# Sigmoid attention and a SiLU block in one kernel: a quad's seven rounds of values put into one burst between its score tiles

## The chip, the cores and the metric

The kernel runs on one core of a Trainium2 chip. Its time is the device time of one launch in microseconds. A difference is stated against the median of the runs of the kernel before.

## The reference

```python
# q, k, v: (8, 12, 448, 64); w_in: (768, 2048); w_out: (2048, 768)
scores = q @ k.transpose(0, 1, 3, 2) / sqrt(64) - log(448)
attn = sigmoid(scores) @ v                      # (8, 12, 448, 64)
x = attn.transpose(0, 2, 1, 3).reshape(3584, 768)
h = x @ w_in
out = (h * sigmoid(h)) @ w_out                  # (3584, 768), float32
```

## The kernel before

There are two kinds of work, and both are mostly matmuls. The kernel writes the order of every engine's instructions by hand, so what stands in the Python program is the order on each engine.

**Attention.** The twelve heads of a batch are worked in three *quads* of four heads, 24 quads in all. A quad has seven *score tiles* (`scores`): a tile is four matmuls of 64 rows by 64 columns (L178) that run in the four quarters of the array, and one sigmoid of 128x896 on ScalarE (L185) that reads the tile `psc` from PSUM and writes `attnT`. `psc` has two buffers of two banks each (`ps_sc`), `attnT` has twelve. When the quad's tiles are there, its *values* (`values`) follow: seven *rounds* of four 64x64 matmuls (L209) that add up in two PSUM tiles `pav`. After the last round VectorE writes both to `xT` (L225). For odd batches from 3 on, four subtractions `xs` follow on VectorE (L273), two `attnT` buffers are held for them until they are read. `pav` shares the four single banks of `ps_1` with all dense products.

**Dense work.** `h_unit` (batches 0 and 1, tile `ph`) and `h_pair` (batches 2 to 7 in pairs, tiles `hx`, `hy`, `hz`, L320; `hy` is in `ps_sc`) make the hidden layer with 128x128 matmuls. `out_set` makes 256 output rows by seven products `po` of eight matmuls (L465) each; VectorE adds them into `osb` (L475), and ScalarE makes one copy `m` a set (L483). These are generators, chained by `all_moe`: each `yield` hands back the price of one matmul in ns (189 or 163).

**The order.** Score tiles and values are placed by the main loop at the end of the kernel; between them `stretch(ns)` draws dense matmuls from the generator until they have cost `ns`. A run of score and value matmuls between two dense matmuls is called a *burst* here. From tile 42 on (the third batch) there are three *stages*: the tiles of two batches, and four of the next, are spread over the dense work that lies ahead of the next `h_pair`, which itself has no bursts. In a stage the kernel before does this for each pair of tiles:

```python
for u in burst:            # two tiles
    scores(*u)
had = values_if_any()      # the waiting quad's first four rounds, or its last three
rows_if_any()              # one kr or qr copy and its DMA transpose, for a later quad
```

and then a stretch of dense work. Its length is the dense time left in the stage, shared over the bursts left, less 200 ns for each round that the burst had. So a quad's values take two bursts, and the two `pav` tiles stay open over the dense stretch between them. In the last stage the rounds that are left after the last pair make bursts of their own.

`after_values` issues the loads of later `v` rows from POOL, `rows_of_quad` the loads of later `k` and `q` rows and the DMA transposes from SP.

Of the kernel before, what the change touches and what calls it, by code (L numbers as in the profile page):

```python
# [3 lines left out]

# [9 lines left out]
AF = mybir.ActivationFunctionType  # L14
# [4 lines left out]
def kernel(  # L19
# [9 lines left out]
    nc = tc.nc  # L29

    B, H, S, D = q.shape
# [4 lines left out]
    NCH = S // HP  # L36
    NPAIR = H // 2
    NQ = NPAIR // 2
    NT_B = NQ * NCH
    NCC = DMODEL // P  # L40
    NFC = DFF // P
    NO2 = DMODEL // 2
    NQB = NQ * B
    NHC = NFC // 2
# [54 lines left out]
    warm = cpool.tile([P, 1], F32, tag="warm", name="warm")  # L99
# [69 lines left out]
    def scores(g, ch, unread=0):  # L169
        attnT[g, ch] = p12.tile([P, 2, S], F16, tag="attnT", name="attnT")  # L170
        psc = ps_sc.tile([P, 2, 512], F32, tag="pssc", name="psc")
        for _ in range(unread):
            nc.tensor.matmul(psc[:, 0, :P], dummy[:, :P], dummy[:, :P], start=True, stop=True)  # L173
        for half in range(2):
            own = slice(half * HP, (half + 1) * HP)
            for j in range(2):
                rows = slice(j * D, (j + 1) * D)
                nc.tensor.matmul(  # L178
                    psc[own, j, :S],
                    qkT["k", g][rows, ch, own],  # L180
                    qkT["q", g][rows, :, own],
                    start=True,
                    stop=True,
                )
        nc.scalar.activation(  # L185
            attnT[g, ch], psc[:, :, :S], AF.Sigmoid, bias=NEG_LOG_S, scale=QKSCALE
        )
# [3 lines left out]
    h_done = set()  # L191
# [3 lines left out]
    def values(g, end=NCH):  # L195
        b, iq = divmod(g, NQ)
        if b not in xT:
            assert b < 2 or b - 2 in h_done
            xT[b] = p2.tile([P, NPAIR, S], F16, tag="xT", name="xT")
        pav, done_rounds = part_of.pop(g, None) or (  # L200
            [ps_1.tile([P, 512], F32, tag="ps1", name="pav") for _ in range(2)],
            0,
        )
        for ch in range(done_rounds, end):
            at = attnT.pop((g, ch))
            for half in range(2):
                own = slice(half * HP, (half + 1) * HP)
                for j in range(2):
                    nc.tensor.matmul(  # L209
                        pav[half][j * D : (j + 1) * D, :S],  # L210
                        flat["v", g][own, j, ch, :],
                        at[own, j, :],
                        start=(ch == 0),
                        stop=(ch == NCH - 1),
                    )
        if end < NCH:
            part_of[g] = pav, end
            return
        for half in range(2):
            if b > 2 and b % 2 == 1 and iq == NQ - 1 and half == 0:  # L220
                nc.scalar.activation(
                    xT[b][:, half * NQ + iq, :], pav[half][:, :S], AF.Copy, scale=SX
                )
            else:
                nc.vector.tensor_scalar_mul(xT[b][:, half * NQ + iq, :], pav[half][:, :S], SX)  # L225
        if b > 2 and b % 2 == 1:
            x_sums(b // 2, iq)
        if iq == NQ - 1:
            ready.add(b)
# [32 lines left out]
    HCC = NCC // 2  # L262
# [296 lines left out]
    def all_moe():  # L559
        for m in range(B // 2):  # L560
            tail = []
            if m == 0:
                yield from moe_h(0)
                yield from moe_h(1)
                tail = [None, *first_sg]
            else:
                yield from h_pair(m, tail)
            yield from moe_set(m, 0, tail)
            yield from moe_set(m, 2)
            yield from moe_set(m, 4)  # L570
            if m % 2 == 1:
                g = NCH - 1
                yield from out_set(
                    kept,
                    row_blocks(m - 1, g),
                    block(g),
                    row_blocks(m, g),
                    1.0,
                    last=(m == B // 2 - 1),
                )  # L580

    stream = all_moe()
    done = due = 0.0

    def stretch(ns):
        nonlocal done, due
        due += ns
        while done < due or hold:
            step_ns = next(stream, None)
            if step_ns is None:  # L590
                break
            done += step_ns
# [19 lines left out]
    units = [(g, ch) for g in range(NQB) for ch in range(NCH)]  # L612
    waiting = []
# [11 lines left out]
    def after_values(g):  # L625
        if g == 0:
            load("v", 3)
            load_w_in(2)
            load_w_in(3)
        elif g == 1:  # L630
            load("v", 4)
            load_w_out(1, 0)
            load_w_out(1, 1)
        elif g == 2:
            load("v", 5)
            load("kq", 6)
            load_w_out(0, 1)
            load("kq", 7)
            load_w_out(0, 0)
        elif 4 < g < NQB - 3:  # L640
            load("v", g + 3)

    later = []
    seen = cpool.tile([1, 1], F16, tag="seen", name="seen")

    def rows_of_quad(g, name, copy):
        dma_transpose(g, name, copy)
        if name == "q" and g + 3 < NQB:
            nc.gpsimd.tensor_copy(seen, qkT["q", g][:1, NCH - 1, P - 1 :])  # L649
            if g == 6:  # L650
                load("v", 6)
                load("kq", 8)
                load("v", 7)
            load("kq", g + 3)

    def rows_if_any():
        if later:
            rows_of_quad(*later.pop(0), nc.vector.tensor_copy)

    def values_if_any():  # L660
        if not waiting:
            return 0
        g, begin, end = waiting.pop(0)
        rounds(g, end)
        return end - begin
# [10 lines left out]
    def transposes(g, name):  # L676
        pe_transpose(g, ((name, 0, 4), (name, 4, NCH)))
        if name == "q":
            after_transpose(g)

    def rounds(g, end):
        values(g, end)
        if end == NCH:
            after_values(g)
# [31 lines left out]
        for _ in range(4):  # L716
            next(unit)

    PACE, BURST, ROUND, SPARE = 1600, 590, 200, 2400
    sets = 7 * NHC * 163  # L720
    h_at = [(2 * NFC * NCC - 8) * 189 + 3 * sets]
    for m in (1, 2):
        h_at.append(h_at[-1] + 7 * NHC * HCC * 189 + (3 + m % 2) * sets)
    AHEAD = 4
    ends = [2 * NT_B, 4 * NT_B + AHEAD, 6 * NT_B + AHEAD, 8 * NT_B]
    values_left = 2 * NT_B
    stretch(PACE)
    for n in range(NT_B + 3, len(units), 2):
        burst = units[n : n + 2]
        if n == 2 * NT_B:  # L730
            values_if_any()
            stretch(13500)
            later.extend(((8, "k"), (8, "q")))
        for u in burst:
            scores(*u)
        had = values_if_any()
        rows_if_any()
        for g, ch in burst:
            if ch == NCH - 3 and g >= 6 and g % 6 < 4 and g + 3 < NQB:
                later.extend(((g + 3, "k"), (g + 3, "q")))  # L740
            if ch == NCH - 1:
                waiting.extend(((g, 0, NCH),) if n < 2 * NT_B else ((g, 0, 4), (g, 4, NCH)))
        if n in (30, 32):
            transposes(5, "kq"[n // 2 - 15])
        if n < ends[0]:
            stretch(PACE)
            continue
        m = bisect.bisect(ends, n)
        if n + 2 == ends[m]:
            nc.scalar.activation(warm, warm, AF.Silu)  # L750
        dense = h_at[m - 1] - SPARE - done
        due = done
        stretch((dense + values_left * ROUND) / ((ends[m] - n) // 2) - had * ROUND)
        values_left -= had
        if n + 2 == ends[m]:
            while waiting:
                values_if_any()
                stretch(SPARE / 3)
            values_left = 2 * NT_B
            while 2 * m not in h_done:  # L760
                done += next(stream)
            due = done
            stretch(3000)
    for _ in stream:
        pass

# [29 lines left out]
```

## Time and profile before

| | |
|---|---|
| median of 3 runs | 366.58 us (366.13 to 366.73) |
| the profiled execution | 366.59 us |
| its span, first to last instruction | 364.8 us |
| TensorE matmuls, busy | 358.0 us, 98% of the span |
| VectorE, ScalarE, GpSimd, busy | 264.0, 248.3, 63.7 us |
| stages with bursts of the changed loop | about 76 to 123, 159 to 212, 248 to 292 us |

In the rows of the timeline the first number is the start in us from the span's start, the second the time from the first start to the last end of the merged instructions, then engine, line, operation, output and inputs, shape and count; a bracket gives idle time of the engine just before and what ended it. PE is TensorE's matmuls, PEld its weight loads, DVE VectorE, ACT ScalarE, POOL GpSimd, SP the sync engine's queue. Matmuls are pipelined and their ends are modelled, so rows of neighbours overlap.

### The profile page before, as it was taken

To read this page: it belongs to the slowest core of one execution; us is meant where nothing else is said; L and a number is where in the kernel's file an instruction comes from. 1 tells how busy PE (TensorE), PEld (TensorE's weight loads), DVE (VectorE), ACT (ScalarE), POOL (GpSimd) and SP (SyncE) were. 2 spreads that over 40 slices of the span, in tenths; PEclk is the share of its full clock that TensorE was granted. 3 is DMA by queue.
4 is the path that set the end of the run, shared out by engine and by line. 5 is a ranking of instruction groups with operands and counts; after the bars stand their busy time and mean duration, and the time that the engine had idled before them with its cause. 6 is when DMAs were issued, how large, how long until landed. Compare 5 with 4: busy or idle time off the path is not lost.

```text
span 364.8 us, 7652 instructions
## 1 busy us (share of the span) xinstructions
PE 358.0 (98%) x3023; PEld 181.5 (50%) x3023; DVE 264.0 (72%) x497; ACT 248.3 (68%) x362; POOL 63.7 (17%) x105
## 2 busy tenths in 40 slices
PE   8999999999999999999999999999999999999995
PEld 4554445444444555554444455554444455556663
DVE  2574679976888587877668677886867577778773
ACT  4997886787878677587677768658878756660000
POOL 8544310603241002002024101100100000000000
PEclk9999999999999999999999999999999999999999
DMA  8999999999999436307999953812854020003333
GB/s 133 199 205 205 205 204 188 167 185 133 214 156 216 90 81 102 50 0 142 141 173 140 199 115 53 127 25 46 169 78 112 18 71 0 3 0 88 86 86 86
DMA packets 65314, 42.78 MB, mean 117 GB/s; under 512 B 35968, under 2 KB 61824, under 8 KB 65280
## 3 DMA queue, kind: packets, MB, share of 16 engines
q0 software_dynamic: 26944, 22.58, 42.9%
q1 hardware_dynamic: 38112, 19.41, 26.4%
q8 instruction: 23, 0.38, 0.4%
q10 hardware_dynamic: 224, 0.33, 0.2%
q14 instruction: 11, 0.09, 0.1%
HBM read 45.61 MB, written 11.01 MB: 155 GB/s over the span
## 4 chain that ended last, share of the span: by engine, by line
PE 91%; ACT 4%; DVE 2%; DMA 1%; issue 1%; DVEq 0%
PE po L465 36%; PE hy L320 11%; PE psc L178 10%; PE ph L244 9%; PE pav L209 8%; PE hz L320 7%; PE hx L320 7%; ACT attnT L185 4%; DMA qs<-in_q_dram 1%; DVE xs L273 1%; PE ptrq L147 1%; PE ptrk L147 0%; DVE osb L475 0%; PE psc L173 0%; DVE xT L225 0%
## 5 line engine op out<-in xcount | busy, mean ns | idle before, releaser
L185 ACT ACTIVATE attnT<-psc 128x896 f16<-128x896 f32 x168 | 144.1, 930 | 31.7 <-PE psc L178 31.4
L465 PEld LDWEIGHTS <-S 128*128 128x128 f16 x448 | 41.1, 98 | 36.4 <-issue 11.8
L475 DVE SCALAR_TENSOR_TENSOR osb<-po,osb 128x384 f32<-128x384 f32 x70 | 37.6, 554 | 19.4 <-PE po L465 18.8
L178 PE MATMUL psc<-qT,kT 64*64 64x448 f16 x672 | 50.7, 363 | 0.7 <-ACT attnT L185 0.4
L225 DVE TENSOR_SCALAR xT<-pav 128x448 f16<-128x448 f32 x45 | 26.1, 620 | 27.3 <-PE pav L209 27.3
L331 ACT ACTIVATE gTr<-u 128x448 f16<-128x448 f32 x48 | 27.6, 575 | 23.1 <-DVE u L344 19.1
L465 PE MATMUL po<-T,S 128*128 128x384 f16 x224 | 41.6, 327 | 0.0
L465 PE MATMUL po<-w_out_sb,S 128*128 128x384 f16 x224 | 41.5, 327 | 0.0
L209 PE MATMUL pav<-attnT,vf 64*64 64x448 f16 x672 | 41.1, 350 | 0.3 <-DVE gTr L257 0.2
L320 PEld LDWEIGHTS <-w_in_sb 128*128 128x128 f16 x288 | 28.2, 98 | 26.4 <-issue 0.4
L465 PEld LDWEIGHTS <-gTr 128*128 128x128 f16 x304 | 28.0, 98 | 25.6 <-issue 8.6
L244 PE MATMUL ph<-xT,w_in_sb 128*128 128x448 f16 x192 | 38.8, 353 | 0.0
L465 PE MATMUL po<-w_out_sb,gTr 128*128 128x384 f16 x192 | 36.6, 327 | 0.0
L320 PE MATMUL hy<-xs,w_in_sb 128*128 128x448 f16 x144 | 35.1, 352 | 0.1
L320 PE MATMUL hx<-xT,w_in_sb 128*128 128x448 f16 x144 | 34.6, 352 | 0.0
L320 PEld LDWEIGHTS <-W 128*128 128x128 f16 x216 | 21.1, 98 | 19.6
L178 PEld LDWEIGHTS <-kT 64*64 64x64 f16 x672 | 15.8, 104 | 29.5 <-issue 26.9
L84 POOL DMA_DIRECT2D vf<-in_v_dram x24 | 17.0, 712 | 59.0 <-PE pav L209 53.3
L244 PEld LDWEIGHTS <-w_in_sb 128*128 128x128 f16 x192 | 17.6, 98 | 19.4 <-issue 4.1
L475 DVE SCALAR_TENSOR_TENSOR osb<-po,m 128x384 f32<-128x384 f32 x42 | 22.9, 552 | 5.5 <-PE psc L178 2.0
L257 DVE TENSOR_TENSOR gTr<-ph,tsig 128x448 f16<-128x448 f32 x32 | 19.7, 621 | 9.9 <-ACT tsig L256 9.6
L649 POOL COPY seen<-qT 1x1 f16<-1x1 f16 x15 | 3.9, 257 | 127.7 <-DMA qT<-qr 127.7
(75 smaller groups left out, 433.7 us busy)
## 6 DMA issues: line engine op xcount, KB each, us to landing
out_dram<-osb SPq DMA_DIRECT2D x54, 192.0 KB, 3.0
vf<-in_v_dram POOLq DMA_DIRECT2D x24, 224.0 KB, 7.5
kf<-in_k_dram POOLq DMA_DIRECT2D x23, 224.0 KB, 4.9
qf<-in_q_dram POOLq DMA_DIRECT2D x23, 224.0 KB, 7.2
w_in_sb<-in_moe_w_in_dram POOLq DMA_DIRECT2D x8, 384.0 KB, 12.3
w_out_sb<-in_moe_w_out_dram POOLq DMA_DIRECT2D x4, 768.0 KB, 17.3
kT<-kr SPq DMA_TRANSPOSE x18, 4.7
qT<-qr SPq DMA_TRANSPOSE x18, 3.1
```

What stands on the lines that cost most here:

```text
L84: nc.gpsimd.dma_start(flat[name, g][:, :, c0:c1].rearrange("p j c d -> p j (c d)"), rows_in(name, g)[:, :, c0 * D : c1 * D],)
L178: nc.tensor.matmul(psc[own, j, :S], qkT["k", g][rows, ch, own], qkT["q", g][rows, :, own], start=True, stop=True,)
L185: nc.scalar.activation(attnT[g, ch], psc[:, :, :S], AF.Sigmoid, bias=NEG_LOG_S, scale=QKSCALE)
L209: nc.tensor.matmul(pav[half][j * D : (j + 1) * D, :S], flat["v", g][own, j, ch, :], at[own, j, :], start=(ch == 0), stop=(ch == NCH - 1),)
L225: nc.vector.tensor_scalar_mul(xT[b][:, half * NQ + iq, :], pav[half][:, :S], SX)
L244: nc.tensor.matmul(ph[:, :S], w_in_of[:, cc // NQ, cc % NQ, fc * P : (fc + 1) * P], xT[b][:, cc, :], start=(at == 0), stop=(at == NCC - 1),)
L257: nc.vector.tensor_mul(gTr[:, fc, (b % 2) * S : (b % 2) * S + S], ph[:, :S], tsig)
L320: nc.tensor.matmul(ps, a[:, c, i * P : (i + 1) * P], bs(c), start=(first and c == 0), stop=(c == HCC - 1), skip_group_check=True,)
L331: nc.scalar.activation(gTr[:, side * NHC + i, odd * S : (odd + 1) * S], src, AF.Silu, scale=ISX)
L465: nc.tensor.matmul(po[:, :NO2], a[:, fc, :], w[:, fc, :], start=(fc == 0), stop=(fc == NHC - 1))
L475: nc.vector.scalar_tensor_tensor(out=o, in0=po, scalar=sign * scale, in1=x, op0=ALU.mult, op1=ALU.add)
L649: nc.gpsimd.tensor_copy(seen, qkT["q", g][:1, NCH - 1, P - 1 :])
```

## The change

The loop up to tile 42 stays as it was (it is only written out anew). From there on:

- The bursts of a stage are planned ahead by `bursts_to`: two tiles a burst, and three in the burst after the one that holds a quad's last tile. This third kind carries all seven rounds of that quad, between its second and its third tile. Seven tiles make 2 + 2 + 3, three bursts a quad. A burst that only has values follows where the tiles of the kernel have run out.
- Dense work is dealt by tiles: of what is left in the stage a burst gets the share of its tiles among the tiles left, less what the burst itself is priced at (200 ns, and 190 ns for each tile and round).
- `xT`, `xs`, loads and copies are the same instructions; they move with the rounds and bursts that issue them.

```diff
-    PACE, BURST, ROUND, SPARE = 1600, 590, 200, 2400
+    PACE, SWITCH, TILE, ROUND, SPARE = 1600, 200, 190, 190, 2400
...
-        for u in burst:
-            scores(*u)
-        had = values_if_any()
-        rows_if_any()
-        for g, ch in burst:
-            if ch == NCH - 3 and g >= 6 and g % 6 < 4 and g + 3 < NQB:
-                later.extend(((g + 3, "k"), (g + 3, "q")))
-            if ch == NCH - 1:
-                waiting.extend(((g, 0, NCH),) if n < 2 * NT_B else ((g, 0, 4), (g, 4, NCH)))
...
-        m = bisect.bisect(ends, n)
-        if n + 2 == ends[m]:
-            nc.scalar.activation(warm, warm, AF.Silu)
-        dense = h_at[m - 1] - SPARE - done
-        due = done
-        stretch((dense + values_left * ROUND) / ((ends[m] - n) // 2) - had * ROUND)
-        values_left -= had
-        if n + 2 == ends[m]:
-            while waiting:
-                values_if_any()
-                stretch(SPARE / 3)
-            values_left = 2 * NT_B
-            while 2 * m not in h_done:
-                done += next(stream)
-            due = done
-            stretch(3000)
+    def bursts_to(n, stop):
+        bursts, full = [], None
+        while n < stop or full is not None:
+            burst = units[n : min(n + (2 if full is None else 3), stop)]
+            bursts.append((burst, full))
+            n += len(burst)
+            full = next((g for g, ch in burst if ch == NCH - 1), None)
+        return bursts
...
+    for m in range(1, B // 2):
+        stop = min(2 * (m + 1) * NT_B + 4, len(units))
+        bursts = bursts_to(n, stop)
+        n = stop
+        costs = [
+            SWITCH + TILE * len(burst) + ROUND * NCH * (full is not None) for burst, full in bursts
+        ]
+        for at, (burst, full) in enumerate(bursts):
+            if full is None:
+                for u in burst:
+                    scores(*u)
+            else:
+                for u in burst[:2]:
+                    scores(*u)
+                rounds(full, NCH)
+                for u in burst[2:]:
+                    scores(*u)
+            rows_if_any()
+            for g, ch in burst:
+                if ch == NCH - 3 and g % 6 < 4 and g + 3 < NQB:
+                    later.extend(((g + 3, "k"), (g + 3, "q")))
+            if at == len(bursts) - 1:
+                nc.scalar.activation(warm, warm, AF.Silu)
+                break
+            due = done
+            tiles = sum(len(burst) for burst, _ in bursts[at:])
+            left = h_at - SPARE - done + sum(costs[at:])
+            stretch(max(left * len(burst) / tiles - costs[at], 0))
+        while 2 * m not in h_done:
+            done += next(stream)
+        due = done
+        stretch(3000)
+        h_at += 7 * NHC * HCC * 189 + (3 + m % 2) * sets
```

More of the change, by code (lines that the diff above doesn't have):

```diff
@@ L1 @@
-import bisect
 import math
@@ L717 @@
             next(unit)
-    PACE, BURST, ROUND, SPARE = 1600, 590, 200, 2400
[L720 to L725, printed above, removed]
-    values_left = 2 * NT_B
+    PACE, SWITCH, TILE, ROUND, SPARE = 1600, 200, 190, 190, 2400
     stretch(PACE)
-    for n in range(NT_B + 3, len(units), 2):
+    for n in range(NT_B + 3, 2 * NT_B, 2):
@@ L729 @@
         burst = units[n : n + 2]
-        if n == 2 * NT_B:
-            values_if_any()
-            stretch(13500)
-            later.extend(((8, "k"), (8, "q")))
         for u in burst:
             scores(*u)
-        had = values_if_any()
-        rows_if_any()
+        values_if_any()
         for g, ch in burst:
-            if ch == NCH - 3 and g >= 6 and g % 6 < 4 and g + 3 < NQB:
-                later.extend(((g + 3, "k"), (g + 3, "q")))
             if ch == NCH - 1:
-                waiting.extend(((g, 0, NCH),) if n < 2 * NT_B else ((g, 0, 4), (g, 4, NCH)))
+                waiting.append((g, 0, NCH))
@@ L743 @@
         if n in (30, 32):
             transposes(5, "kq"[n // 2 - 15])
-        if n < ends[0]:
-            stretch(PACE)
-            continue
-        m = bisect.bisect(ends, n)
-        if n + 2 == ends[m]:
-            nc.scalar.activation(warm, warm, AF.Silu)
-        dense = h_at[m - 1] - SPARE - done
-        due = done
-        stretch((dense + values_left * ROUND) / ((ends[m] - n) // 2) - had * ROUND)
-        values_left -= had
-        if n + 2 == ends[m]:
-            while waiting:
-                values_if_any()
-                stretch(SPARE / 3)
-            values_left = 2 * NT_B
-            while 2 * m not in h_done:
-                done += next(stream)
-            due = done
-            stretch(3000)
+        stretch(PACE)
@@ new lines @@
+    values_if_any()
+    stretch(13500)
+    later.extend(((8, "k"), (8, "q")))
+    def bursts_to(n, stop):
[6 more added lines that the diff above has]
+        return bursts
+    sets = 7 * NHC * 163
+    h_at = (2 * NFC * NCC - 8) * 189 + 3 * sets
@@ new lines @@
+    n = 2 * NT_B
+    for m in range(1, B // 2):
[28 more added lines that the diff above has]
+            done += next(stream)
+        due = done
+        stretch(3000)
+        h_at += 7 * NHC * HCC * 189 + (3 + m % 2) * sets
```

## The prediction

> **What bounds the kernel now.** I read the page first: the busy shares, the clock row and the chain that ended last.
>
> ```profile
> span 364.8 us, 7652 instructions
> ...
> PE 358.0 (98%) x3023; PEld 181.5 (50%) x3023; DVE 264.0 (72%) x497; ACT 248.3 (68%) x362; POOL 63.7 (17%) x105
> ...
> PEclk9999999999999999999999999999999999999999
> ...
> PE 91%; ACT 4%; DVE 2%; DMA 1%; issue 1%; DVEq 0%
> ```
>
> TensorE is busy 98% of the span, its clock is never cut, and 91% of the chain is matmuls. So the time is the length of TensorE's stream, and a change gains only what it takes out of that stream: matmuls, waits, or lost time between matmuls. The number of matmuls doesn't change here. What is left is the price of going from the dense 128x128 matmuls (`po`) to the 64x64 ones (scores `psc`, values `pav`) and back. For that I read the timeline of TensorE in the second stage with attention, where nothing waits.
>
> ```profile
> 164.33 0.57 PE L178 MATMUL psc<-qT,kT 64*64 64x448 f16 x8
> 164.74 0.93 PE L209 MATMUL pav<-attnT,vf 64*64 64x448 f16 x16
> 165.59 1.31 PE L465 MATMUL po<-w_out_sb,S 128*128 128x384 f16 x7
> 166.84 0.57 PE L178 MATMUL psc<-qT,kT 64*64 64x448 f16 x8
> 167.24 0.74 PE L209 MATMUL pav<-attnT,vf 64*64 64x448 f16 x12
> 167.91 0.34 PE L465 MATMUL po<-w_out_sb,S 128*128 128x384 f16 x1
> 168.08 1.30 PE L465 MATMUL po<-w_out_sb,gTr 128*128 128x384 f16 x7
> 169.31 0.57 PE L178 MATMUL psc<-qT,kT 64*64 64x448 f16 x8
> 169.82 1.64 PE L465 MATMUL po<-w_out_sb,gTr 128*128 128x384 f16 x9
> 171.29 0.65 PE L465 MATMUL po<-T,S 128*128 128x384 f16 x3
> 171.87 0.57 PE L178 MATMUL psc<-qT,kT 64*64 64x448 f16 x8
> ```
>
> The first column is the start. The ends overlap, since matmuls are pipelined, so I use starts alone. Nine `po` matmuls go from 169.82 to 171.29: 1.47 / 9 = 0.163 each. Four 64x64 matmuls (one score tile, or one round of values) run together as a group. Call a group's price G and the price of one burst's two changes C. From 164.33 to 166.84 there are 2 tiles, 4 rounds and 7 dense: 2.51 - 7 x 0.163 = 1.37 = 6G + C. From 169.31 to 171.87 there are 2 tiles and 12 dense: 2.56 - 12 x 0.163 = 0.60 = 2G + C. The difference gives G = 0.19, and C = 0.22. The stretch between them (2 tiles, 3 rounds, 8 dense, 2.47) gives C = 0.21 with that G. So each burst of small matmuls costs 0.22 us beyond its work, whatever lies in it.
>
> Weight loads show what the 0.22 is:
>
> ```profile
> 164.33 0.14 PEld L178 LDWEIGHTS <-kT 64*64 64x64 f16 x8 [0.32 <-issue]
> ```
>
> ```profile
> 165.59 0.93 PEld L465 LDWEIGHTS <-S 128*128 128x128 f16 x7 [0.36 <-issue]
> ```
>
> At both edges the load path stands idle for 0.32 and 0.36 us and waits for nothing: the first load of the other kind isn't taken ahead of the running matmuls.
>
> The Trainium skill ("TensorE: Matmul & The Clock Gate", Part 3, The mechanism) says that a weight load overlaps with running matmuls only where their row groups differ, and a 128-row load meets all of them; the trace agrees, by the idle 0.32 and 0.36 at each edge. The Trainium skill, on the same page under LDWEIGHTS (loading the stationary operand), prices a load at its columns over 1.2 GHz, which would make the two edges 0.05 + 0.11 = 0.16 us, an estimate, and nine bursts 1.4 us; the rows above say 0.22.
>
> **The change part by part.** *Fewer bursts.* From tile 42 on there are 126 score tiles. Before, they come in 63 pairs, the values of a quad ride behind two of them (four rounds, then three), and the last quad's values make two bursts of their own: 65. After, a quad takes a pair, a pair, and a triple with all seven rounds of the quad before between its second and third tile: by the loop 20 bursts in the first stage, 18 in the second, 18 in the third (among them one single tile and one of values alone), 56 in all. The order of TensorE's instructions in the two built programs says the same, 90 and 81 such stretches over the whole kernel. 9 x 0.22 = 1.98 us come out of the stream. The starts are rounded to 0.01, which leaves C between 0.20 and 0.23: 1.8 to 2.1.
>
> *A new crossing, values to scores, inside 17 bursts.* The stages in question have none. The first part of the kernel does:
>
> ```profile
> 22.34 0.38 PE L178 MATMUL psc<-qT,kT 64*64 64x448 f16 x4
> 22.55 0.74 PE L209 MATMUL pav<-attnT,vf 64*64 64x448 f16 x12
> 23.13 0.38 PE L178 MATMUL psc<-qT,kT 64*64 64x448 f16 x4
> ```
>
> Three rounds and the crossing take 23.13 - 22.55 = 0.58, which is three groups of 0.19 and 0.01 over. So 17 crossings cost 17 x 0.01 = 0.2 at most, and I take 0.
>
> *The third tile's buffer.* There are two score buffers, so the third tile of a burst waits until ScalarE has read the first.
>
> ```profile
> 163.02 0.91 ACT L185 ACTIVATE attnT<-psc 128x896 f16<-128x896 f32 x1
> 164.77 1.73 ACT L185 ACTIVATE attnT<-psc 128x896 f16<-128x896 f32 x2 [0.83 <-PE psc L178]
> ```
>
> The sigmoid starts 164.77 - 164.33 = 0.44 after its burst and takes 0.91, so the buffer is free at 1.35. Two tiles and seven rounds take 9 x 0.19 = 1.71: the seven rounds cover the sigmoid with 0.36 to spare. The second sigmoid ends at 0.44 + 1.73 = 2.17, and the third needs about 0.82 more, to 2.99. The next burst follows six to nine dense matmuls later: its first tile at about 9 x 0.19 + 0.19 + 0.22 + 6 x 0.163 = 3.1, its second, which needs the third tile's buffer, at 3.3. Cover remains, 0.3. What eats into it is the 0.50 us copy `m` (L483), one a set, ten in the three stages; here one in the third stage, with the pair that met it:
>
> ```profile
> 276.53 0.64 PE L178 MATMUL psc<-qT,kT 64*64 64x448 f16 x8
> 276.62 0.50 ACT L483 ACTIVATE m<-po 128x384 f32<-128x384 f32 x1
> ```
>
> By the built order of ScalarE four of them come directly ahead of a triple (two in the first stage, two in the third). Each could hold the third tile by 0.50 - 0.36 = 0.14 and the tile after next by 0.2. Bound: 4 x 0.34 = 1.4; below, 0. The pair at 276.53 shows what such a meeting cost before: 0.64 where 0.57 is usual, 0.07. I take 0.2 for all four.
>
> *The waits that the third stage has now.*
>
> ```profile
> 284.91 0.64 PE L178 MATMUL psc<-qT,kT 64*64 64x448 f16 x8
> ...
> 286.05 0.66 PE L465 MATMUL po<-T,gTr 128*128 128x384 f16 x3
> ...
> 288.90 1.39 PE L209 MATMUL pav<-attnT,vf 64*64 64x448 f16 x16
> ...
> 293.72 0.73 PE L320 MATMUL hz<-xs,W 128*128 128x448 f16 x3
> 294.28 0.73 PE L320 MATMUL hx<-xT,w_in_sb 128*128 128x448 f16 x3
> 295.12 0.73 PE L320 MATMUL hy<-xs,w_in_sb 128*128 128x448 f16 x3
> ```
>
> Two pairs (276.53 above and 284.91) take 0.64 for 0.57, 0.14 together, the last quad's first four rounds take 1.39 where 0.93 is usual, 0.46 more, and `hy` comes 0.84 after `hx` where the three matmuls before it took 0.56, 0.28 more. Sum 0.88. The two large ones come from VectorE's queue:
>
> ```profile
> 286.15 1.15 DVE L225 TENSOR_SCALAR xT<-pav 128x448 f16<-128x448 f32 x2 [2.29 <-PE pav L209]
> ...
> 288.75 1.68 DVE L475 SCALAR_TENSOR_TENSOR osb<-po,osb 128x384 f32<-128x384 f32 x3
> ```
>
> After a quad's last round VectorE works off two `xT` and four `xs`, from 286.15 to 288.75, and only then clears the `po` buffers that piled up, which the next values need. Before, the last quad's values come 288.90 - 286.05 = 2.85 us after the end of the quad before. After, the built order has a third tile, 6 dense, a pair, 9 dense, a single, 4 dense between them: 4 groups and 3 C and 19 dense = 0.76 + 0.6 + 3.1 = 4.5 us, more than the same VectorE work (2.6 to 288.75 and three `osb`, 1.68: 4.3). So the 0.46 goes. Behind the last values stand five dense matmuls instead of one ahead of `hx`, 0.65 us more for `xT` and `xs`, so the 0.28 goes too. I take 0.8 of 0.88. If the cover fails, 0.
>
> The same VectorE work now stands behind a whole seven rounds in six quads. But both `pav` buffers are held from their first round to `xT` without a dense stretch in between, 7 x 0.19 = 1.3 us where it was 166.84 - 164.74 + 0.4 + 0.57 = 3.1 us. Two of the four single banks come back sooner for `po`. I take 0 for that, between 0 and 0.5 us.
>
> *Moved along.* The `kr` and `qr` copies and their DMA transposes go one a burst; a quad asks for two and has three bursts (3.5 before), and they are for three quads later. SP's stores and POOL's loads behind them keep their order; the values end a burst earlier, so `vf` loads go out earlier. On the dense side the same 163 ns matmuls are dealt in other portions: 0.
>
> **Sum.** The profiled execution took 366.59 us (span 364.8 and 1.8 around it), as the median of the runs, 366.58. -1.98 - 0.8 + 0.2 = -2.58: **364.0 us**.
>
> **Rivals.** *ScalarE takes part of it back* (chance 0.09): copies and sigmoids in a row hold more third tiles than the four. With the bounds above, +1.4, +0.5 from the `pav` side and the old waits kept in another place (0 instead of -0.8), the sum is 366.59 - 1.8 + 1.9 = 366.7 at the very end; the middle of this case is 365.5. For it, the sum of busy time over the three stages with bursts (76 to 123.5, 159 to 212.5 and 247.8 to 292 us):
>
> ```profile
> sum 145.20, PE 145.13 PEld 69.89 DVE 102.49 ACT 114.16 POOL 25.44; mean PE 48.38 PEld 23.30 DVE 34.16 ACT 38.05 POOL 8.48
> ```
>
> ScalarE is busy 114 of 145 us, so a delay dies out slowly. Against: its work stays the same.
>
> *The third tile waits in every triple* (0.03): slower. It starts where the first sigmoid comes more than 0.36 late, and decides where a triple costs (2.78 + 0.7) / 17 = 0.2 on average. Were each of the 17 late by a whole copy's 0.50 behind a backlog, the third tile would cost 0.14 and the second of the next burst 0.2: 17 x 0.34 = 5.8, and 366.59 - 2.78 + 5.8 = 369.6. Against it: the row at 164.77 has ScalarE idle 0.83 us before a pair, and only ten copies exist. The Trainium skill ("Trainium Kernel Development and Optimization", Best Practices) warns that tiling TensorE speeds up compute but not the emptying of PSUM; the trace agrees so far as sigmoids (0.91 a tile) take longer than scores (0.19), and this rival is what the rule would make of the change.
>
> *The crossing costs as much as a change of kind* (0.03): 17 x 0.22 = 3.7, less 1.98 and 0.8: 367.5, slower. The row at 23.13 speaks against it, but it is of the first part, where the matmuls around it wait for ScalarE anyway.
>
> *The bursts get fewer, the time doesn't* (0.02): if the 0.22 were a pause that TensorE makes up elsewhere, 366.5. Against: the dense pitch is the same 0.163 near bursts and far from them.
>
> **The numbers.** The forecast has 0.83. A difference of 0.2% (0.7 us) is about what a measurement of this kernel can tell from none. Faster by more takes the forecast and 0.08 of the first rival, 0.91; the rest of that rival and the last one are the same, with a little of the slower two that ends near zero, 0.04; slower 0.05. The range: 366.59 - 2.1 - 0.88 = 363.6, and 0.3 of run-to-run spread (366.13 to 366.73) below, 363.3. Above it reaches into the first rival, 365.3.
>
> **What would show it.** Right: 0.22 us between dense `po` and each burst in all 56 bursts; third tiles that start 9 x 0.19 = 1.7 after the first; values of the last quad at 0.19 a round; TensorE's stream shorter by 2.0 in bursts and 0.8 in the third stage. Wrong: `psc` rows above 0.57 for a pair, or more than 0.2 from the last `pav` to the third tile, released by ScalarE; `pav` that wait for VectorE after `xs`.

## The result and the profile after

The changed kernel took 363.75 us against 366.65 us before: a ratio of 0.9923, 95% interval 0.9909 to 0.9937. Taken once more beside later experiments it was 364.02 against 366.39, a ratio of 0.9940 (0.9929 to 0.9952). One of the four executions of the changed kernel took 2028.04 us for a reason that nothing here shows; the ratio leaves it out, and without it the median is 363.52. So the gain is between 2.4 and 3.1 us; 2.58 and 364.0 us were forecast.

The page of the profile of the changed kernel, the same lines as before:

```profile
span 361.7 us, 7653 instructions
...
PE 355.1 (98%) x3023; PEld 182.7 (50%) x3023; DVE 264.1 (73%) x497; ACT 248.7 (69%) x362; POOL 62.8 (17%) x105
...
PE 93%; ACT 4%; DVE 1%; issue 1%; DVEq 0%
```

The instructions are as many but for one, the other engines as busy as before to within 1 us; TensorE's busy time is 2.9 us shorter, and the chain is matmuls still more than before. The profiled execution took 363.52 us, 3.07 less than the one before, but not all of that is the change. Up to tile 42 both kernels do the same, and the first `ph` after the opening stood at 26.27 us before and at 25.91 after. That 0.36 is a difference between two executions at the start: in the second trace of the changed kernel the same `ph` stands at 26.30. From that point to the end, the two window rows (of before, then of after; behind the window stand its length, then busy time and count of PE, PEld, DVE, ACT and POOL, then the clock, the DMA share and GB/s):

```profile
26.27:364.80 338.53, 333.94 (x2676) 168.49 (x2672) 250.43 (x472) 226.69 (x335) 46.95 (x76) 1.00 0.67 113
```

```profile
25.91:361.70 335.79, 331.42 (x2676) 169.84 (x2672) 250.72 (x472) 227.12 (x335) 46.21 (x77) 1.00 0.67 114
```

338.53 - 335.79 = 2.74 us is the change's own part in these two executions; in the second trace of the changed kernel the starts of the matmuls from the first `ph` to the last agree with the first within 0.01 us. Where it comes from is read from TensorE's timeline of the second stage. One triple, and two pairs:

```profile
163.03 0.57 PE L177 MATMUL psc<-qT,kT 64*64 64x448 f16 x8
163.44 1.49 PE L208 MATMUL pav<-attnT,vf 64*64 64x448 f16 x28
164.76 0.36 PE L177 MATMUL psc<-qT,kT 64*64 64x448 f16 x4
165.05 1.64 PE L464 MATMUL po<-w_out_sb,S 128*128 128x384 f16 x9
166.62 0.57 PE L177 MATMUL psc<-qT,kT 64*64 64x448 f16 x8
167.12 0.34 PE L464 MATMUL po<-w_out_sb,S 128*128 128x384 f16 x1
167.30 1.79 PE L464 MATMUL po<-w_out_sb,gTr 128*128 128x384 f16 x10
169.01 0.57 PE L177 MATMUL psc<-qT,kT 64*64 64x448 f16 x8
```

From 163.03 to 166.62 there are ten groups and nine dense matmuls: 3.59 - 1.47 - 10 x 0.19 = 0.22. The pair behind it, with 11 dense: 169.01 - 166.62 - 1.79 - 0.38 = 0.22. A triple with seven rounds pays no more for its two changes than a pair. The third tile starts 1.73 us after the first (1.71 forecast), and ScalarE takes the three in one run, 0.44 after the burst's start:

```profile
163.47 2.62 ACT L184 ACTIVATE attnT<-psc 128x896 f16<-128x896 f32 x3 [0.67 <-PE psc L177]
```

The end of the third stage, where before the pairs took 0.64, the last values 1.39 for four rounds and `hy` came 0.28 late:

```profile
283.81 0.57 PE L177 MATMUL psc<-qT,kT 64*64 64x448 f16 x8
...
286.95 1.52 PE L208 MATMUL pav<-attnT,vf 64*64 64x448 f16 x28
288.40 0.99 PE L464 MATMUL po<-w_out_sb,S 128*128 128x384 f16 x5
289.22 1.30 PE L319 MATMUL hx<-xT,w_in_sb 128*128 128x448 f16 x6
290.36 0.73 PE L319 MATMUL hy<-xs,W 128*128 128x448 f16 x3
```

Seven rounds in 1.52 and `hy` 1.14 after `hx` (six times 0.19): these waits are gone. New is a wait in the last triples of stages one and two, here stage one:

```profile
117.05 0.57 PE L177 MATMUL psc<-qT,kT 64*64 64x448 f16 x8
117.45 1.49 PE L208 MATMUL pav<-attnT,vf 64*64 64x448 f16 x28
117.92 1.73 ACT L184 ACTIVATE attnT<-psc 128x896 f16<-128x896 f32 x2 [0.74 <-PE pav L208]
118.89 0.38 PE L177 MATMUL psc<-qT,kT 64*64 64x448 f16 x4
```

The third tile comes 1.84 after the first, not 1.73, and the first sigmoid 0.87 after its tile, not 0.44 to 0.50 as in the other triples. What ended its wait is a round of values. With seven tiles of the full quad, one of the next and four buffers of `xs` held, the twelve `attnT` buffers are taken, and a round has to give one back. The dense matmuls go on 2.16 after the burst's start, not 2.02: it costs 0.14 us, twice.

Added up by the starts: nine bursts give 1.98, the waits that are gone 0.96 (0.84 of them those that the forecast put at 0.88), the new ones take 0.33 back (the two of 0.14 and five pairs 0.01 late). That is 2.6 of the 2.69 us by which the last matmul starts sooner behind the first `ph`; the remaining 0.08 isn't placed.

### The profile page after: what moved, and what is told of

The parts are those of the page before. It is cut to its first block, busy times and chain, and to the rows that moved or that the text cites. A ratio compares the mean times of both kernels' runs of the same rounds, so it can differ in the third digit from the quotient of the medians.

```text
span 361.7 us, 7653 instructions
## 1 busy us (share of the span) xinstructions
PE 355.1 (98%) x3023; PEld 182.7 (50%) x3023; DVE 264.1 (73%) x497; ACT 248.7 (69%) x362; POOL 62.8 (17%) x105
## 4 chain that ended last, share of the span: by engine, by line
PE 93%; ACT 4%; DVE 1%; issue 1%; DVEq 0%
PE po L464 37%; PE hy L319 11%; PE psc L177 10%; PE ph L243 10%; PE pav L208 8%; PE hx L319 8%; PE hz L319 8%; ACT attnT L184 4%; PE pw L133 1%; PE ptrk L146 0%; PE ptrq L146 0%; ACT tsig L255 0%; DVE W L283 0%; DVE gTr L256 0%; DVE osb L474 0%
## 5 line engine op out<-in xcount | busy, mean ns | idle before, releaser
L177 PE MATMUL psc<-qT,kT 64*64 64x448 f16 x672 | 52.0, 362 | 0.8 <-ACT attnT L184 0.4
L474 DVE SCALAR_TENSOR_TENSOR osb<-po,osb 128x384 f32<-128x384 f32 x70 | 37.6, 553 | 16.2 <-PE po L464 15.4
L208 PE MATMUL pav<-attnT,vf 64*64 64x448 f16 x672 | 37.6, 349 | 0.2 <-DVE gTr L256 0.2
L177 PEld LDWEIGHTS <-kT 64*64 64x64 f16 x672 | 16.7, 104 | 28.7 <-issue 24.8
L208 PEld LDWEIGHTS <-vf 64*64 64x64 f16 x672 | 20.1, 107 | 11.6 <-issue 1.6
```

What stands on the lines that cost most here:

```text
L177: nc.tensor.matmul(psc[own, j, :S], qkT["k", g][rows, ch, own], qkT["q", g][rows, :, own], start=True, stop=True,)
L208: nc.tensor.matmul(pav[half][j * D : (j + 1) * D, :S], flat["v", g][own, j, ch, :], at[own, j, :], start=(ch == 0), stop=(ch == NCH - 1),)
L474: nc.vector.scalar_tensor_tensor(out=o, in0=po, scalar=sign * scale, in1=x, op0=ALU.mult, op1=ALU.add)
```

## The experiments

Theory A is the one of the prediction: each burst costs 0.22 us, and the rounds cover the third tile's wait. Against it stood five others. B: the gain is the values in one go. C: a burst's price is a pause that is made up elsewhere. D: the gain is the dealing by tiles. E: the number of bursts alone counts, not the order inside. F: inside a triple only the distance from the first to the third tile counts. A last one, G, is about loads that land late, and comes up at the end.

**The values in one go, pairs kept** (edit to the kernel before):

```diff
-                waiting.extend(((g, 0, NCH),) if n < 2 * NT_B else ((g, 0, 4), (g, 4, NCH)))
+                waiting.append((g, 0, NCH))
```

> The kernel before with one edit: a quad's seven rounds ride together behind one pair of tiles instead of four and three behind two; pairs stay pairs, so 88 bursts in the whole kernel where there were 90 (and 81 after the change). Theory A (the time goes with the number of bursts, 0.22 us each): 2 x 0.22 = 0.4 us less than before, and up to 0.9 us more of the third stage's waits may go or stay: 365.3 to 366.3 us. Rival B (the gain comes from the values in one go: the two PSUM tiles of values held for 1.3 us instead of 3.1, VectorE relieved): most of the 2.9 us is gained here too, 363.8 to 364.5 us.

365.71 us against 366.5, a ratio of 0.9991 (0.9968 to 1.0014), which can't be told from no change; the interval allows a gain of 1.2 us at most. By the starts of all matmuls in the trace the stream from the first `ph` on is 1.0 us shorter than before: two bursts (0.44) and a part of the third stage's waits. The rest of the gain isn't here, so B falls. The same trace shows on what the third stage's largest wait hangs:

```profile
284.68 0.37 PE L178 MATMUL psc<-qT,kT 64*64 64x448 f16 x4
...
289.01 1.52 PE L209 MATMUL pav<-attnT,vf 64*64 64x448 f16 x28
```

The first row stands right behind the rounds of the quad before. The last values start 4.33 us behind it, where the kernel before had 2.85, and run at full pace.

**The very last quad's values in one burst, nothing else** (edit to the kernel before):

```diff
-                waiting.extend(((g, 0, NCH),) if n < 2 * NT_B else ((g, 0, 4), (g, 4, NCH)))
+                waiting.extend(((g, 0, NCH),) if n < 2 * NT_B or g == NQB - 1 else ((g, 0, 4), (g, 4, NCH)))
```

> The kernel before with one edit: the seven rounds of the very last quad come in one burst of their own, where they made two with five dense matmuls between; all else, pairs and split values included, stays. 89 bursts for 90. Theory A: one burst less, 0.22 us; the wait of 0.46 us at the last quad's first rounds stays, since they come as soon after the quad before as they did (2.85 us, VectorE needs 4.3); the wait of 0.28 us at hy goes, since six dense matmuls follow the values instead of one. Together 0.5 us less than before, 366.0 us. If the wait of 0.46 belongs to the split, not to VectorE's queue, it goes too: 365.6 us.

365.88 us against 366.39, a ratio of 0.9986 (0.9977 to 0.9994): 0.5 us, as expected, and the parts are seen apart:

```profile
288.68 1.96 PE L209 MATMUL pav<-attnT,vf 64*64 64x448 f16 x28
...
293.83 0.73 PE L320 MATMUL hx<-xT,w_in_sb 128*128 128x448 f16 x3
294.40 0.73 PE L320 MATMUL hy<-xs,w_in_sb 128*128 128x448 f16 x3
```

Seven rounds take 1.96 where the changed kernel has 1.52: the 0.44 stays, since the values come as soon behind VectorE's queue as before. `hy` follows `hx` at 0.57: that wait goes with the dense matmuls between (six ahead of `hx`, where it was one).

**One more change of kind in each triple** (edit to the changed kernel; the dense matmul is moved, not added):

```diff
                 for u in burst[:2]:
                     scores(*u)
+                if burst:
+                    done += next(stream)
                 rounds(full, NCH)
```

> The changed kernel with one dense matmul of 0.163 us moved from the stretch behind each triple to a place between its second tile and its rounds. The work is the same, the cover of the third tile is longer; 17 bursts are cut in two, 98 instead of 81. Theory A: 17 x 0.22 = 3.7 us more than the changed kernel, 367.5 us, and each cut shows 0.22 us in the trace. Rival C (a burst's price is a pause made up elsewhere, and the gain has another source): within 0.5 us of the changed kernel, 363.3 to 364.3 us.

368.57 us, 4.8 over the 363.75 of the change; 3.7 was expected. The rows of the first triple:

```profile
79.15 0.57 PE L177 MATMUL psc<-qT,kT 64*64 64x448 f16 x8
79.65 0.34 PE L464 MATMUL po<-w_out_sb,gTr 128*128 128x384 f16 x1
79.92 1.52 PE L208 MATMUL pav<-attnT,vf 64*64 64x448 f16 x28
81.27 0.36 PE L177 MATMUL psc<-qT,kT 64*64 64x448 f16 x4
81.56 0.99 PE L464 MATMUL po<-w_out_sb,gTr 128*128 128x384 f16 x5
```

From 79.15 to 81.56 there are ten groups and one dense matmul: 2.41 - 1.90 - 0.16 = 0.35, where a whole triple has 0.12 (163.03 to 165.05: 2.02 - 1.90). The difference, 0.23, is the price of a burst again, within the rounding. 17 of 0.22 make 3.7; by the starts in the trace the stream is 4.55 us longer than the changed kernel's, most of the rest being waits in other places (0.16 and 0.2 at two pairs near stage ends, 0.26 in a later `hz`). The price is per change of kind, and nothing makes it up elsewhere: C falls.

**Where the rounds lie.** Three edits to the changed kernel leave the bursts at 81. The rounds behind the third tile:

```diff
-                for u in burst[:2]:
+                for u in burst if full % 6 < 5 else burst[:2]:
                     scores(*u)
                 rounds(full, NCH)
-                for u in burst[2:]:
+                for u in burst[2:] if full % 6 == 5 else ():
```

> The changed kernel with the seven rounds behind the third tile instead of ahead of it, in 15 of the 17 triples (the last triples of stages one and two stay as they are, since their tiles need the buffers that the rounds give back). Bursts stay at 81. Theory A (the rounds cover the first tile's sigmoid): the third tile has its turn 0.4 us after the first and its buffer at 1.4: 1.0 us of wait each, 15 us more, 378 us. Rival E (the number of bursts alone counts, where the rounds lie is indifferent): 363.5 to 364.5 us.

379.91 us, 16.2 over the change.

```profile
79.61 0.57 PE L177 MATMUL psc<-qT,kT 64*64 64x448 f16 x8
80.05 2.54 ACT L184 ACTIVATE attnT<-psc 128x896 f16<-128x896 f32 x3 [0.45 <-PE psc L177]
81.01 0.38 PE L177 MATMUL psc<-qT,kT 64*64 64x448 f16 x4 [0.83 <-ACT attnT L184]
```

The third tile starts 1.40 after the first, released by ScalarE; two tiles alone would have put it at 0.40. That is the 1.0 us that the seven rounds cover (1.06 where the sigmoid starts 0.50 after its tile), 15 times. E falls.

Four rounds ahead of the third tile and three behind it:

```diff
-                rounds(full, NCH)
+                rounds(full, 4 if burst else NCH)
                 for u in burst[2:]:
                     scores(*u)
+                if burst:
+                    rounds(full, NCH)
```

> The changed kernel with four rounds ahead of the third tile and three behind it, in one burst. Bursts stay at 81. Theory A: the third tile has its turn at 6 x 0.19 + 0.02 = 1.16 us and its buffer at 1.40: 0.24 us in each of 17 triples, 4.1 us more, 367.8 us. Rival E: 363.5 to 364.5 us.

369.78 us, 6.0 over the change where 4.1 was expected.

```profile
79.24 0.57 PE L177 MATMUL psc<-qT,kT 64*64 64x448 f16 x8
79.64 0.93 PE L208 MATMUL pav<-attnT,vf 64*64 64x448 f16 x16
79.67 2.54 ACT L184 ACTIVATE attnT<-psc 128x896 f16<-128x896 f32 x3 [0.46 <-PE psc L177]
80.64 0.38 PE L177 MATMUL psc<-qT,kT 64*64 64x448 f16 x4
```

The third tile again starts at 1.40. By starts, the wait is 0.27 in triples like this one, 0.33 where the sigmoid begins 0.50 instead of 0.44 after its tile, and 0.71 in the last triples of stages one and two, whose first sigmoid waits for a buffer anyway. Four rounds are too few.

The rounds between the first and the second tile:

```diff
-                for u in burst[:2]:
+                for u in burst[:1]:
                     scores(*u)
                 rounds(full, NCH)
-                for u in burst[2:]:
+                for u in burst[1:]:
```

> The changed kernel with the seven rounds between the first and the second tile of a triple. Bursts stay at 81, and the third tile still comes nine groups after the first. Theory A: no wait inside the triple, but the second and third sigmoid end later (about 2.9 and 3.7 us after the start, instead of 2.2 and 3.0), and the second tile of the next pair needs the third's buffer: with 6 and 7 dense matmuls between (nine or ten triples) it waits 0.46 and 0.3 us, with 9 (five) not at all; about 3.4 us more than the changed kernel, 367 us, with the waits at the second tile of the pair. Rival F (only the distance from the first to the third tile counts): 363.5 us.

367.37 us, 3.6 over the change.

```profile
81.89 0.55 PE L177 MATMUL psc<-qT,kT 64*64 64x448 f16 x8
...
83.61 0.85 PE L177 MATMUL psc<-qT,kT 64*64 64x448 f16 x8
```

The first row is the triple's last two tiles, the last the pair behind it. The triple runs through; the pair takes 0.85 where 0.57 is usual, 0.28 of wait. In the pairs with seven dense matmuls between it is 0.28 to 0.34, with six 0.50, with nine none that counts, ten pairs in all: as worked out ahead. F falls: the place between second and third tile serves two waits, the third tile's and that of the next pair.

**Dense work dealt evenly over bursts** (edit to the changed kernel):

```diff
-            stretch(max(left * len(burst) / tiles - costs[at], 0))
+            stretch(max((left - sum(costs[at:])) / sum(len(b) > 0 for b, _ in bursts[at:]), 0))
```

> The changed kernel with the dense work dealt evenly over bursts instead of by tiles (7 to 9 dense matmuls behind pairs and triples alike, where it was 9 to 11 behind pairs and 6 to 9 behind triples). Bursts stay at 81. Theory A: 363.5 to 364.3 us, as the changed kernel or a few tenths more, since pairs now follow each other at 0.6 + 7 x 0.163 = 1.7 us where ScalarE needs 1.73 for two sigmoids, and the copies of 0.5 us have no room. Rival D (dealing by tiles is what gives the gain): over 365 us.

365.51 us, 1.8 over the change, against an expectation of at most 0.5 from theory A. Two pairs of the third stage, with ScalarE:

```profile
255.57 0.57 PE L177 MATMUL psc<-qT,kT 64*64 64x448 f16 x8
256.08 1.47 PE L464 MATMUL po<-w_out_sb,S 128*128 128x384 f16 x8
257.48 0.69 PE L177 MATMUL psc<-qT,kT 64*64 64x448 f16 x8
```

```profile
256.01 1.73 ACT L184 ACTIVATE attnT<-psc 128x896 f16<-128x896 f32 x2 [0.80 <-PE psc L177]
```

The pair's second buffer is free at 0.44 + 1.73 = 2.17 after the pair's start. With eight dense matmuls the next pair's second tile has its turn at 257.48 + 0.19 - 255.57 = 2.1, too soon, and the pair takes 0.69. With nine it would be 2.26. So waits come back, 1.3 us at seven pairs and 0.8 in three triples of this trace. D is half right: the dealing gains nothing of itself (this kernel still beats the one before, at 0.9981, 0.9971 to 0.9990), but without it two thirds of the gain are lost.

**The changed kernel's two remaining places.** The wait at the stage ends, with the rounds one tile sooner there:

```diff
-                for u in burst[:2]:
+                ahead = 1 if full % 6 == 5 and full < NQB - 1 else 2
+                for u in burst[:ahead]:
                     scores(*u)
                 rounds(full, NCH)
-                for u in burst[2:]:
+                for u in burst[ahead:]:
```

> The changed kernel with the rounds between the first and the second tile in the last triples of stages one and two alone. There the first sigmoid starts 0.87 us after its tile instead of 0.44, with the first round of values as what ended its wait: its output buffer is free only after that round. The third tile is 0.14 us late for it, twice. Theory A: the first round comes 0.2 us sooner, so both waits go and no pair follows that could suffer: 0.28 us less than the changed kernel, 363.4 us. If the first sigmoid waits for something else: no change, 363.7 us.

363.63 us, ratio 0.9927 (0.9914 to 0.9939): not told apart from the change. In its trace the 0.14 is gone in stage two; in stage one 0.15 at the pair ahead and 0.12 in the triple took its place, in an execution in which VectorE waited 1.25 us there for a store of `osb` to leave. Whether that always comes isn't settled by one trace.

Triples from tile 24 on. The plan starts there, where the values of quads 3 and 4 rode behind pairs; with it the dense work between bursts goes from 1600 to 1800 ns, and the transposes of quad 5 come a burst later:

```diff
-    for n in range(NT_B + 3, 2 * NT_B, 2):
...
+    for burst, full in bursts_to(NT_B + 3, 2 * NT_B):
+        for u in burst[:2]:
+            scores(*u)
+        if full is not None:
+            rounds(full, NCH)
+        for u in burst[2:]:
+            scores(*u)
...
+        if burst:
+            stretch(PACE * 9 / 8)
```

> The changed kernel with its plan of bursts used from tile 24 on as well: the values of quads 3 and 4 go between the second and the third tile of a triple there too, dense work between bursts 1800 instead of 1600 ns, the transposes of quad 5 a burst later. 80 bursts instead of 81. Theory A: 0.22 us less for the burst, and the waits of the two value bursts there go (0.14 and 0.61 us beyond the 0.22 in the trace of the changed kernel, at 33 and 45 us, where the last round waits for the sigmoid of the tile just ahead of it): 363.75 - 0.97 = 362.8 us. If these waits only move behind the next burst: 363.5 us.

363.3 us, with single runs from 362.8 to 366.5. It was taken again:

> Triples from tile 24 on, once more. Its runs lay between 362.8 and 366.5 us. Theory A for the low end: one burst and two waits less, 0.97 us under the changed kernel, 362.8 us. Theory G for the high end: it needs the sums over w_out about 1 us sooner, and in runs where the loads of w_out land late VectorE waits for them (2.8 us in the profile of the slow one): single runs of 365 us and above come back. If neither, 363.3 us in all runs.

363.5 us beside 364.02 for the change, single runs from 362.7 to 367.6. Both together with the stage ends:

> Triples from tile 24 on, and the rounds between the first and second tile in the last triples of stages one and two. Theory A: what the two gave apart, 0.97 and 0.14 to 0.28 us: 362.6 us, with single runs above 365 us if theory G holds.

362.97 us, the lowest median; ratio to before 0.9918 (0.9894 to 0.9941), single runs 362.35 to 365.67. By these intervals it isn't told apart from the changed kernel (0.9929 to 0.9952 beside it). In its trace the stream from the first `ph` on is 1.3 us shorter than the changed kernel's. The waits it removes stand in the changed kernel like this:

```profile
45.02 0.57 PE L177 MATMUL psc<-qT,kT 64*64 64x448 f16 x8
45.42 0.36 PE L208 MATMUL pav<-attnT,vf 64*64 64x448 f16 x2
46.02 1.33 PE L208 MATMUL pav<-attnT,vf 64*64 64x448 f16 x24 [0.24 <-DVE gTr L256]
```

and the values of the same quad in the version with both edits run at full pace:

```profile
44.31 0.57 PE L177 MATMUL psc<-qT,kT 64*64 64x448 f16 x8
44.71 1.49 PE L208 MATMUL pav<-attnT,vf 64*64 64x448 f16 x28
```

(The row names VectorE; the two `pav` tiles there share banks with `ph`, and VectorE's product, which ends at 45.96, clears one. So the larger of the two waits, 0.61, which I had put down in the expectation to a sigmoid, was a bank.) The high runs of the early triples are seen in the profile of one of 367.25 us:

```profile
65.16 0.56 DVE L433 TENSOR_TENSOR w_out_sb<-w_out_sb 128x768 f16<-128x768 f16 x1 [2.57 <-DMA w_out_sb<-in_moe_w_out_dram]
...
103.01 0.56 DVE L474 SCALAR_TENSOR_TENSOR osb<-po,m 128x384 f32<-128x384 f32 x1 [3.35 <-DMA out_dram<-osb]
...
118.89 0.38 PE L177 MATMUL psc<-qT,kT 64*64 64x448 f16 x4 [1.56 <-DMA qT<-qr]
```

The `w_out` load comes late, as theory G has it, and by the starts the next dense matmuls lose 0.64 us. As much is lost 40 us further on, where VectorE waits for a store and the values for VectorE (0.60), and more where a transpose lands late (1.75). In the profile of the first series, one of 365.49 us, the same three places cost 0.87, 0.79 and 0.74. Whether the first causes the others, or all are one spell of slow transfers, stays open. The version at 362.97 isn't free of it.

## Why the prediction was right

- *Fewer bursts, 9 x 0.22.* Right: the price is 0.22 in triples as in pairs, and it comes back 17 times when 17 changes are put in. This is 2.0 of the 2.7 us. What the 0.22 consists of no run shows. The idle 0.32 and 0.36 of the load path at the edges fit the reading that a load can't overlap a matmul in the same rows, but inside a dense stretch it does: at 165.77 in the kernel before, a 128-row load and the 128-row matmul ahead of it start within 0.01 us. So that rule alone isn't the reason.
- *The crossing from values to scores costs nothing.* Right: ten groups and 0.22 account for the whole triple. In the changed kernel nothing else waits there, which answers the doubt about the row of the first part.
- *The third tile's cover.* Right, and sharper than forecast: the buffer is free at 1.40 (1.35 was worked out from the sigmoid's end; the hand-over is 0.05 more), the tile's turn is at 1.73. In nine of the 17 triples the sigmoid starts 0.50 after its tile, not 0.44, which leaves 0.27 to spare; that was not foreseen and costs nothing here.
- *The old waits of the third stage, -0.8.* They are gone. The 0.46 hangs on the distance behind the quad before: it stayed at 2.85 us with the split gone, and went at 4.33 and in the changed kernel (4.51; 4.5 was worked out). The 0.28 hangs on the dense matmuls ahead of `hx`, as the working had it.
- *The price of the new waits, +0.2.* The size was near by luck, for the cause was wrong. The four copies `m` ahead of a triple cost nothing that shows; 0.28 came from `attnT` buffers at two stage ends, a third resource that the prediction didn't look at.
- *"Dealt in other portions: 0."* Right in its size, incomplete in its reason. It is 0 because by tiles a pair gets at least nine dense matmuls behind it and a triple needs only six. Dealt evenly it would have been +1.8, and no rival of the prediction had that.
- *The rivals.* The third tile that waits in each triple happens only if too few rounds stand ahead of it: four were too few (6 us over the change), none cost 16 us, and by 1.40 us and 0.19 a round six should do, which is an estimate. By the Trainium skill ("Trainium Kernel Development and Optimization", Best Practices), tiling doesn't speed up the emptying of PSUM; the trace agrees where the cover is taken away (1.0 us a triple) and shows no cost where it stands.

## What to carry to other kernels

Where two kinds of matmul share TensorE, measure the price of a change of kind from starts alone (two stretches with different contents give two equations, for the price of a group and that of a change) and then count changes; work doesn't get cheaper, but bursts can get fewer. A burst may grow by whatever its buffers allow, and the work without a reader on the slow engine (here the rounds) belongs just ahead of the part that waits for a buffer. Then deal the filler (here the dense matmuls) by what each burst owes the engine that empties PSUM, or the waits move to the next burst.

## What the runs showed of the hardware

- The hand-over of a PSUM buffer from ScalarE to TensorE took 0.05 us: in the two kernels where it waits, the third tile starts at 1.40, and the sigmoid that held its buffer ends at 0.44 + 0.91.
- A 64x64 burst pays 0.22 us whether it has 2 groups or 10, and a round after a score or a score after a round pays nothing that can be measured: of the changes in this kernel only the one between 64x64 and 128x128 costs.
- The opening differs by some tenths between executions of the same instructions (the first `ph` at 26.27 before, at 25.91 and 26.30 in two traces of the changed kernel), so 0.36 of the 3.1 us between the two spans isn't the change.
